# The last output product in two column halves, and which queues carry the last stores

## The chip, the cores and the metric

The kernel runs on one core of a Trainium2 chip. The metric is the time of one execution on the device in microseconds (us); the time before is the median of three runs. The profile belongs to one further execution, and its span, counted from the first instruction to the last, is a few microseconds shorter than the time.

## The reference

What is computed is a linear attention with a cosine weighting, followed by a feed-forward layer with a swish gate:

```python
q_p, k_p = phi(q, cos_w, sin_w), phi(k, cos_w, sin_w)      # relu(x)*cos, relu(x)*sin, side by side
kv  = np.einsum('bhsf,bhsd->bhfd', k_p, v)
num = np.einsum('bhsf,bhfd->bhsd', q_p, kv)
den = np.einsum('bhsf,bhf->bhs', q_p, k_p.sum(axis=2))[..., None] + 1e-06
x   = (num / den).transpose(0, 2, 1, 3).reshape(4608, 512)
h   = x @ w_in                                              # 4608 x 2048
out = (h * (1.0 / (1.0 + np.exp(-beta * h)))) @ w_out       # 4608 x 512, float32
```

There are 8 batches, 8 heads, 576 positions and 64 dimensions per head. Only the last product, `g @ w_out`, matters for the change.

## The kernel before

The 4608 rows of `x` are done in nine chunks of 512 rows (`c` from 0 to 8). For each chunk the first product and the gate give tiles `g_t` in bf16, and the second product multiplies them with `wout`. From chunk 2 on the second product is done by a fast 2 x 2 block scheme with seven block products instead of eight (`o_fast`). It works on a pair of row tiles of 128 rows, `pr` and `pr + 2`, and on two column halves of `HM` = 256 columns. The seven products are called 1 to 7; each is eight matmuls of 128 rows by 256 columns (line 552). They add up in three PSUM banks, `b_ps`, `e_ps` and `a_ps`. In between, ScalarE copies partial sums out (c1, c5, cu), and VectorE adds them to other banks (a2, a3, a7).

- `o1`, the upper row tile, is complete after a2 (left half, line 602) and a3 (right half, line 603).
- `o2`, the lower row tile, is complete after a7 (right half, line 604) and c4 (left half, line 571 to 576). Product 4 is the last one, and adds to `b_ps`, which c4 then copies.

Nothing reorders the work: the order in which the program issues it is written out by hand, in the strings `ORDER` and `ORDER_END`, which the function `chunk` walks through. `ORDER_END` is used for chunk 8. There `x` and `y` are the two calls of `o_fast`, and `oy3`, `o3y`, `oy4`, `c4y` at its end stand for product 3, a3, product 4 and c4 of the second pair. Each engine takes its instructions in that order, and waits on semaphores for data of the others. Two engines' accesses to the same PSUM bank are ordered one after the other by such waits too, even where they touch different columns.

A finished row tile is written to the output by `store` (line 512), in two transfers of 64 rows each, since each 64 rows belong to another place of the output. Chunks 0 to 6 use GpSimd's queue, the others SyncE's. In chunk 8 the odd row tiles, which are `o1` and `o2` of the second pair, use SyncE's queue for one transfer and ScalarE's for the other. The queue of an engine is in order too: ScalarE can't start a copy before it has issued the transfers that stand ahead of it.

For the last pair, c4 is cut in two: ScalarE copies columns 0 to 127 and VectorE columns 128 to 255 of the same bank, and then both transfers of the left half are issued. After the last store every engine goes through the closing instructions of the program, which the profile shows under line 1058: a drain, and a barrier in which SyncE waits for the transfers to land, and GpSimd gathers all engines.

Of the kernel before, what the change touches and what calls it, by code (L numbers as in the profile page):

```python
# [22 lines left out]
def kernel(  # L23
# [14 lines left out]
    nc = tc.nc  # L38

    B, H, S, D = q.shape  # L40
    DM = H * D
    DF = moe_w_in.shape[1]
    JT = DF // P
    MI = DM // P
    TCH = 512
    NTC = B * S // TCH
# [38 lines left out]
    HM = DM // 2  # L85
    w_e, w_o = wout[:, 0:JT:2], wout[:, 1:JT:2]
    B11, B12, B21, B22 = w_e[:, :, 0:HM], w_e[:, :, HM:DM], w_o[:, :, 0:HM], w_o[:, :, HM:DM]
    T1, T2, T4 = (const.tile([P, JT // 2, HM], BF16, name=f"T{i}") for i in (1, 2, 4))
# [420 lines left out]

    out_v = out.rearrange("(b p n) m -> b n p m", b=B, n=NQ)  # L510

    def store(c, tt, o_sb, m0=0, m1=DM):
        for hf in range(2):
            bb, n = divmod((c * TCH + tt * P) // HP + hf, NQ)
            eng = nc.gpsimd if c < 7 else (nc.sync, nc.scalar)[hf] if c == NTC - 1 and tt % 2 else nc.sync
            eng.dma_start(out=out_v[bb, n][:, m0:m1], in_=o_sb[hf * HP : (hf + 1) * HP, m0:m1])  # L516

    def o_mm(c, tt, jts, cols=1):
        o_ps = ps[:, (2, 3, 0, 1)[tt] if c == 0 else 2 + tt % 2]
        for jt in jts:  # L520
            w = DM // cols if jt > 0 else DM
            for m0 in range(0, DM, w):
                nc.tensor.matmul(o_ps[:, m0 : m0 + w], lhsT=gs[c, jt // 4][:, jt % 4, tt * P : (tt + 1) * P],  # L523
                                 rhs=wout[:, jt, m0 : m0 + w],
                                 start=(jt == 0), stop=(jt == JT - 1 and m0 == DM - w))
        if jts[-1] < JT - 1:
            return
        o_sb = osb_pool.tile([P, DM], FP32, name="o_sb", tag="o_sb")
        nc.scalar.copy(o_sb, o_ps)
        store(c, tt, o_sb)  # L530
# [6 lines left out]
    def late(c):  # L537
        made[c] = made.get(c, 0) + 1
        return made[c] > 14 - SPLITS.get(c, (0, 0))[1]

    def o_fast(c, pr, banks):

        b_ps, e_ps, a_ps = (ps[:, k_, 0:HM] for k_ in banks)
        tok = slice(pr * P, (pr + 1) * P)
        last = c == NTC - 1 and pr == 1

        def prod(dst, left, right, start, stop, pieces=False):
            order = (0, 1, 2, 3, 4, 5, 7, 6) if c + 1 >= B else range(JT // 2)
            for i in order:
                w = HM // 2 if i and pieces else HM  # L550
                for m in range(0, HM, w):
                    nc.tensor.matmul(dst[:, m : m + w], lhsT=left(i), rhs=right[:, i, m : m + w],  # L552
                                     start=start and i == 0,
                                     stop=stop and i == order[-1], skip_group_check=True)

        def g_part(r, hf):
            def at(i):
                jt = 2 * i + r
                return gs[c, jt // 4][:, jt % 4, hf * (TCH // 2) + pr * P : hf * (TCH // 2) + (pr + 1) * P]
            return at  # L560

        def s_part(t):
            return lambda i: t[:, i, tok]

        o1 = osb_pool.tile([P, DM], FP32, name="o_sb", tag="o_sb")
        o2 = osb_pool.tile([P, DM], FP32, name="o_sb", tag="o_sb")
        p1 = part.tile([P, HM], FP32, name="p1", tag="p1")
        p5 = part.tile([P, HM], FP32, name="p5", tag="p5")
        u = part.tile([P, HM], FP32, name="u", tag="u")

        def c4():
            h = HM // 2 if last else HM
            nc.scalar.copy(o2[:, 0:h], b_ps[:, 0:h])
            if last:
                nc.vector.tensor_copy(o2[:, h:HM], b_ps[:, h:HM])
                store(c, pr + 2, o2, 0, HM)

        def stored(key, op):
            def do():
                op()  # L580
                waits[key[0]].discard(key[1:])
                if not waits[key[0]] and not (last and key[0] == "2"):
                    store(c, pr + (2 if key[0] == "2" else 0), o2 if key[0] == "2" else o1)
                if last and key == "2a7":
                    store(c, pr + 2, o2, HM, DM)
            return do

        waits = {"1": {"a2", "a3"}, "2": {"a7", "c4"}}
        add = dict(op=ALU.add)
        return {  # L590
            "1": lambda: prod(b_ps, g_part(0, 0), B11, True, False, late(c)),
            "5": lambda: prod(e_ps, s_part(S1), T1, True, False, late(c)),
            "6": lambda: prod(b_ps, s_part(S2), T2, False, False, late(c)),
            "2": lambda: prod(a_ps, g_part(1, 0), B21, True, True, late(c)),
            "7": lambda: prod(b_ps, s_part(S3), T3, False, False, late(c)),
            "3": lambda: prod(e_ps, s_part(S4), B22, False, True, late(c)),
            "4": lambda: prod(b_ps, g_part(1, 1), T4, False, True, late(c)),
            "c1": lambda: nc.scalar.copy(p1, b_ps),
            "c5": lambda: nc.scalar.copy(p5, e_ps),
            "cu": lambda: nc.scalar.copy(u, b_ps),  # L600
            "c4": stored("2c4", c4),
            "a2": stored("1a2", lambda: nc.vector.tensor_tensor(o1[:, 0:HM], a_ps, p1, **add)),
            "a3": stored("1a3", lambda: nc.vector.tensor_tensor(o1[:, HM:DM], e_ps, u, **add)),  # L603
            "a7": stored("2a7", lambda: nc.vector.tensor_tensor(o2[:, HM:DM], b_ps, p5, **add)),
        }
# [16 lines left out]
    for bank, n0, n1 in ((6, 0, 5), (7, 5, NQ)):  # L622
        for n in range(n0, n1):
            nc.tensor.matmul(ps[:, bank, (n - n0) * HP : (n - n0 + 1) * HP],
                             lhsT=tan9[0:HP, n : n + 1].to_broadcast([HP, P]), rhs=identf,
# [357 lines left out]
    for c in range(2, NTC):  # L983
        b = c + 1
        parts = (6, 0, 4) if c < FAST else (0, 6, 4)
        xb, yb = ((2, 3, 6), (1 if c == FAST - 1 else 7, 3, 6)) if c < FAST else ((3, 2, 0), (1, 2, 0)) if b < B else ((0, 3, 6), (1, 3, 6))
        x, y = o_fast(c, 0, xb), o_fast(c, 1, yb)
        if c >= FAST:
            chunk(c, b, x, y, parts)
# [73 lines left out]
```

## Time and profile before

| | before |
|---|---|
| time, median of three (lowest, highest) | 280.73 us (279.52, 281.05) |
| span of the profiled execution | 278.1 us |
| granted TensorE clock | 0.999 |
| PE busy | 269.0 us, 97% |
| DVE busy | 209.6 us, 75% |
| ACT busy | 178.0 us, 64% |
| GpSimd busy | 71.1 us, 26% |
| stores of `o_sb` on GpSimd, SyncE, ScalarE | 56, 15, 3 |
| GpSimd's last store starts at | 226.4 us |

The busy time is the sum of an engine's instructions; issuing a transfer counts as busy on no engine but GpSimd. In the lines of the profile PE is the matmul, PEld its weight load, DVE is VectorE, ACT is ScalarE, POOL is GpSimd and SP is SyncE. A q behind an engine's name (SPq, ACTq) stands for its sequencer, which waits and issues transfers while the engine itself is idle. `L516` is line 516 of the kernel, where all output stores are issued, `out<-in` names what is written and read, and x4 counts instructions. Landing is the time at which the last byte of a transfer is known to have arrived.

### The profile page before, as it was taken

How to read it: one execution, taken by the hardware profiler on the slowest of the kernel's cores; microseconds unless marked ns; L12 is line 12 of the kernel's file. 1: busy time of each engine (PE TensorE's matmuls, PEld its weight loads, DVE VectorE, ACT ScalarE, POOL GpSimd, SP SyncE). 2: the span in 40 equal slices, each digit the busy share in tenths (PEclk: the TensorE clock that was granted, in tenths of full speed). 3: DMA queues.
4: the chain of work that ended last, by engine and by line, in shares of the span. 5: the costliest groups of instructions: out<-in, count | busy, mean ns of one | idle time of the engine just before them, and what ended most of it. 6: DMA issues, size and time to landing. Idle time of an engine off the chain costs nothing.

```text
span 278.1 us, 8732 instructions
## 1 busy us (share of the span) xinstructions
PE 269.0 (97%) x3613; PEld 191.8 (69%) x3619; DVE 209.6 (75%) x539; ACT 178.0 (64%) x348; POOL 71.1 (26%) x89
## 2 busy tenths in 40 slices
PE   7799999999999999999999999999999999999993
PEld 6354455445874588549854898788767886888783
DVE  5989968668999596358749995799679779659832
ACT  5778757773137657675767586896685279429911
POOL 1444000616192074106320542007400140000000
PEclk9999999999999999999999999999999999999999
DMA  6999999999989968992899189705400640033006
GB/s 242 377 394 382 392 391 305 367 204 396 213 261 295 266 193 219 384 177 42 184 373 241 35 211 277 147 21 106 116 2 12 116 113 4 0 76 78 0 4 150
DMA packets 50583, 53.98 MB, mean 194 GB/s; under 512 B 31200, under 2 KB 31472, under 8 KB 50544
## 3 DMA queue, kind: packets, MB, share of 16 engines
q1 hardware_dynamic: 47584, 45.82, 57.4%
q0 software_dynamic: 2688, 7.34, 9.0%
q8 instruction: 28, 0.46, 0.7%
q10 hardware_dynamic: 272, 0.27, 0.4%
q14 instruction: 11, 0.09, 0.2%
HBM read 36.71 MB, written 9.44 MB: 166 GB/s over the span
## 4 chain that ended last, share of the span: by engine, by line
PE 91%; DMA 3%; DVE 2%; SPq 1%; issue 1%; ACTq 0%; ACT 0%
PE ps L552 31%; PE ps L380 25%; PE ps L474 11%; PE ps L523 10%; PE ps L428 7%; PE ps L293 4%; DMA raw_v<-in_v_dram 3%; PE ps L272 3%; SPq L79 1%; DVE xs L315 1%; PE ps L234 0%; PE ps L352 0%; DVE win L115 0%; DVE rden L308 0%; DVE vb L209 0%
## 5 line engine op out<-in xcount | busy, mean ns | idle before, releaser
L380 PE MATMUL ps<-xt,win 128*128 128x512 bf16 (+1 forms) x327 | 71.1, 375 | 0.1
L388 ACT ACTIVATE g_t<-ps,beta 128x512 bf16<-128x512 f32 x80 | 54.6, 688 | 19.1 <-PE ps L380 17.9
L380 PEld LDWEIGHTS <-win 128*128 128x128 bf16 x327 | 31.4, 98 | 35.2 <-issue 0.4
L516 POOL DMA_DIRECT2D out_dram<-o_sb x56 | 31.7, 571 | 65.5 <-DVE o_sb L603 33.0
L552 PEld LDWEIGHTS <-S 128*128 128x128 bf16 x476 | 44.3, 98 | 4.7
L419 ACT ACTIVATE g_t<-ps,beta 128x512 bf16<-128x512 f32 x64 | 41.2, 697 | 3.4 <-PE ps L428 2.2
L552 PEld LDWEIGHTS <-g_t 128*128 128x128 bf16 x364 | 33.0, 98 | 3.6
L222 POOL TENSOR_TENSOR qs<-qt,tanr 128x1152 bf16<-128x1152 bf16 x8 | 19.4, 2447 | 46.9 <-DVE S L399 17.2
L399 DVE TENSOR_TENSOR S<-g_t 128x512 bf16<-128x512 bf16 (+1 forms) x62 | 22.3, 393 | 11.5 <-ACT g_t L388 9.1
L523 PE MATMUL ps<-wout,g_t 128*128 128x256 bf16 (+1 forms) x171 | 28.6, 318 | 0.4 <-issue 0.2
L552 PE MATMUL ps<-wout,g_t 128*128 128x256 bf16 (+1 forms) x238 | 28.1, 266 | 0.0
L552 PE MATMUL ps<-wout,S 128*128 128x256 bf16 (+1 forms) x238 | 27.4, 266 | 0.0
L552 PE MATMUL ps<-T,S 128*128 128x256 bf16 (+1 forms) x238 | 27.1, 266 | 0.0
L428 PE MATMUL ps<-xt,win 128*128 128x512 bf16 (+1 forms) x111 | 24.0, 350 | 0.0
L315 DVE TENSOR_TENSOR xs<-ps,rden 128x768 bf16<-128x768 f32 (+4 forms) x26 | 22.8, 884 | 0.8
L523 PEld LDWEIGHTS <-g_t 128*128 128x128 bf16 x177 | 16.9, 98 | 9.2
L219 DVE TENSOR_SCALAR vb<-raw_v,cos 128x256 bf16<-128x256 f32 x63 | 22.6, 417 | 0.0
L217 ACT ACTIVATE vb<-raw_v,sin 128x256 bf16<-128x256 f32 (+1 forms) x50 | 21.8, 498 | 0.8 <-DMA raw_v<-in_v_dram 0.8
L474 PE MATMUL ps<-w_stage 128*128 128x256 bf16 x120 | 20.3, 273 | 0.0
L474 PEld LDWEIGHTS <-w_stage 128*128 128x128 bf16 x160 | 15.5, 98 | 3.9
L222 POOL TENSOR_TENSOR w_stage<-qt,tanr 128x1152 bf16<-128x1152 bf16 x4 | 9.4, 2380 | 27.9 <-DVE den L304 27.9
L428 PEld LDWEIGHTS <-win 128*128 128x128 bf16 x111 | 10.9, 98 | 6.7
(104 smaller groups left out, 380.3 us busy)
## 6 DMA issues: line engine op xcount, KB each, us to landing
raw_v<-in_v_dram SPq DMA_DIRECT2D x7, 1152.0 KB, 10.6
raw_k<-in_k_dram SPq DMA_DIRECT2D x7, 1152.0 KB, 8.3
raw_q<-in_q_dram SPq DMA_DIRECT2D x7, 1152.0 KB, 8.0
out_dram<-o_sb POOLq DMA_DIRECT2D x56, 128.0 KB, 4.6
w_stage<-in_moe_w_in_dram SPq DMA_DIRECT2D x3, 1024.0 KB, 13.4
w_stage<-in_moe_w_out_dram SPq DMA_DIRECT2D x2, 1024.0 KB, 7.9
w_stage<-in_moe_w_out_dram SPq DMA_DIRECT2D x4, 512.0 KB, 12.0
out_dram<-o_sb SPq DMA_DIRECT2D x13, 128.0 KB, 2.4
```

What stands on the lines that cost most here:

```text
L219: nc.vector.tensor_scalar(o, a, scalar1=t[:, n : n + 1], scalar2=None, op0=ALU.mult)
L222: return eng.tensor_tensor(dst.rearrange("q n (g p) -> q n g p", g=2), src.rearrange("q n (g p) -> q n g p", g=2), tanr[:, n0:n1].unsqueez ...
L315: nc.vector.tensor_tensor(o.rearrange("q j n s d -> q j (n s) d"), nv[:, :, a:z, :, 0:D].rearrange("q j n s d -> q j (n s) d"), rden[:, :, ...
L380: nc.tensor.matmul(ps[:, h_bank(c, jt), i * 64 : (i + w) * 64], lhsT=win[jt // 4][:, mi, (jt % 4) * P : (jt % 4 + 1) * P], rhs=xt[:, i : i ...
L388: nc.scalar.activation(gs[c, jt // 4][:, jt % 4], ps[:, h_bank(c, jt)], AF.Silu, scale=beta[:, jt : jt + 1])
L399: return nc.vector.tensor_tensor(o, l, r, op=op)
L419: nc.scalar.activation(gs[c, jt // 4][:, jt % 4], ps[:, bank], AF.Silu, scale=beta[:, jt : jt + 1])
L428: nc.tensor.matmul(ps[:, bank, o * 64 : z * 64], lhsT=win[jt // 4][:, mi, (jt % 4) * P : (jt % 4 + 1) * P], rhs=xt[:, o:z, jp, g * HP : (g ...
L474: nc.tensor.matmul(dst, lhsT=left[:, g], rhs=right[:, :, g * HP : (g + 1) * HP], start=start and g == 0, stop=stop and g == 1, skip_group_ ...
L516: eng.dma_start(out=out_v[bb, n][:, m0:m1], in_=o_sb[hf * HP : (hf + 1) * HP, m0:m1])
L523: nc.tensor.matmul(o_ps[:, m0 : m0 + w], lhsT=gs[c, jt // 4][:, jt % 4, tt * P : (tt + 1) * P], rhs=wout[:, jt, m0 : m0 + w], start=(jt == ...
L552: nc.tensor.matmul(dst[:, m : m + w], lhsT=left(i), rhs=right[:, i, m : m + w], start=start and i == 0, stop=stop and i == order[-1], skip ...
```

## The change

The last product (product 4 of the second pair in chunk 8) is computed in two column halves of 128 columns: eight matmuls for columns 0 to 127, then VectorE copies these and they are stored, on SyncE's and GpSimd's queues; then eight matmuls for columns 128 to 255, which ScalarE copies, with stores on ScalarE's and SyncE's queues. It is for letting the copy and the store of the first half run while the second is still to be computed. The two stores of `o1` of that pair move to GpSimd's queue, so that SyncE's and ScalarE's queues are free for the last ones. The right half of `o2` keeps SyncE and ScalarE.

```diff
-    def store(c, tt, o_sb, m0=0, m1=DM):
+    def store(c, tt, o_sb, m0=0, m1=DM, engs=None):
         for hf in range(2):
             bb, n = divmod((c * TCH + tt * P) // HP + hf, NQ)
-            eng = nc.gpsimd if c < 7 else (nc.sync, nc.scalar)[hf] if c == NTC - 1 and tt % 2 else nc.sync
+            eng = nc.gpsimd if c < 7 else nc.sync
+            if engs:
+                eng = engs[hf]
...
-        def c4():
-            h = HM // 2 if last else HM
-            nc.scalar.copy(o2[:, 0:h], b_ps[:, 0:h])
-            if last:
-                nc.vector.tensor_copy(o2[:, h:HM], b_ps[:, h:HM])
-                store(c, pr + 2, o2, 0, HM)
-
         def stored(key, op):
             def do():
                 op()
                 waits[key[0]].discard(key[1:])
+                if last and key == "2a7":
+                    store(c, pr + 2, o2, HM, DM, (nc.sync, nc.scalar))
                 if not waits[key[0]] and not (last and key[0] == "2"):
-                    store(c, pr + (2 if key[0] == "2" else 0), o2 if key[0] == "2" else o1)
-                if last and key == "2a7":
-                    store(c, pr + 2, o2, HM, DM)
+                    store(c, pr + (2 if key[0] == "2" else 0), o2 if key[0] == "2" else o1,
+                          engs=(nc.gpsimd, nc.gpsimd) if last else None)
             return do
+
+        def prod_last():
+            left, right, h = g_part(1, 1), T4, HM // 2
+            for m in (0, h):
+                for i in range(JT // 2):
+                    nc.tensor.matmul(b_ps[:, m : m + h], lhsT=left(i), rhs=right[:, i, m : m + h], start=False,
+                                     stop=m > 0 and i == JT // 2 - 1, skip_group_check=True)
+                if m == 0:
+                    nc.vector.tensor_copy(o2[:, 0:h], b_ps[:, 0:h])
+                    store(c, pr + 2, o2, 0, h, (nc.sync, nc.gpsimd))
+
+        def copy_last():
+            h = HM // 2
+            nc.scalar.copy(o2[:, h:HM], b_ps[:, h:HM])
+            store(c, pr + 2, o2, h, HM, (nc.scalar, nc.sync))
...
-            "4": lambda: prod(b_ps, g_part(1, 1), T4, False, True, late(c)),
+            "4": prod_last if last else lambda: prod(b_ps, g_part(1, 1), T4, False, True, late(c)),
...
-            "c4": stored("2c4", c4),
+            "c4": copy_last if last else stored("2c4", lambda: nc.scalar.copy(o2[:, 0:HM], b_ps)),
```

## What I expected before the run

> **What bounds the kernel now.** I read the page first: PE is busy for 97% of the span at full granted clock, and the chain that ended last is 91% PE. So the body is TensorE's, and the change leaves it alone: every instruction before the last product is the same on every engine. All that can move is the stretch from the last product to the end of the span. I therefore read the chain of waits in order of time from 270 us on (start, length, what):
>
> ```profile
> 269.95 2.96 PE ps L552 x27
> 272.92 0.02 issue
> 272.94 0.44 DVE o_sb L603
> 273.38 0.02 issue
> 273.40 0.47 ACTq L516
> ...
> 274.04 0.28 ACT o_sb L573
> 274.32 0.02 issue
> 274.34 0.29 DVE o_sb L575
> ```
>
> The reader is to see that the last copies do not wait for PE. The last eight matmuls end at 273.78 (start 272.74 and 1.04 long in the timeline), yet ACT's copy starts at 274.04: ACT's own queue was issuing half of the o1 store (0.47 us), which in turn had waited for the DVE sum L603. Then DVE's copy waits for ACT's. Next, the stores of the end, from the timeline and from the answer for line 516 on SyncE's queue from 273.6 on:
>
> ```profile
> 272.98 2.57 SPq L516 DMA_DIRECT2D out_dram<-o_sb  x4
> ...
> 274.66 0.47 ACTq L516 DMA_DIRECT2D out_dram<-o_sb  x1
> ```
>
> ```profile
> L516 SPq DMA_DIRECT2D out_dram<-o_sb x3: 547/549/605, 273.7 to 275.0; - x3
> ...
> DMA to landing us min/median/max: 2.1/2.5/2.6
> ```
>
> SyncE issues back to back, some 0.65 us apart, so that its last store goes out at 275.0 though its data was ready at 274.63: about 0.35 us of backlog. It lands 2.1 us later, at 277.14; the span ends at 278.06, some 0.9 us after that, in the closing drains and semaphores of line 1058.
>
> Last, line 1058 on GpSimd, between 220 and 235 us, and GpSimd's timeline:
>
> ```profile
> L1058 POOLq DRAIN  x1: 5496/5496/5496, 226.2 to 226.2; - x1
> ```
>
> ```profile
> 223.84 3.08 POOL L516 DMA_DIRECT2D out_dram<-o_sb  x6 [4.24 <-DVE o_sb L603]
> ```
>
> This is the line that decides my forecast. GpSimd's last store starts at 226.40 and its record ends at 226.92. The closing drain behind it runs until 226.16 + 5.50 = 231.66: 4.73 us past the end of that record, and 2.3 us past the landing of the last store (226.4 + 2.9 = 229.3). Now it lies under 46 us of other engines' work and costs nothing. The two other drains of GpSimd, at the very end with no store before them, take 0.10 and 0.04 us.
>
> **What the Trainium skill says.** "DMA: Bandwidth & Descriptors", section "Issuing engines are not separate DMA queues": stores from several engines share the same DMA engines, and spreading them saves only the sequencer's issue time. The trace agrees: an issue takes 0.47 to 0.61 us on SyncE and ScalarE, and that is the backlog above. The same page, "Anatomy of one DMA — SWDGE (gpsimd) path", puts about 2.0 us of fixed cost on a GpSimd transfer, mostly the receipt of the write; the six stores from 223.8 on land after 2.2 to 2.9 us, SyncE's at the end after 2.1 to 2.6. "PSUM — Partial Sum Buffer", section "PSUM bank collisions raise a hardware error", wants accesses of two engines to one bank kept apart even at different columns; the trace shows it kept, DVE's copy of columns 128 to 256 waits for ACT's of 0 to 128. I found no page that prices GpSimd's drain behind stores.
>
> **The change part by part.**
>
> 1. *Product in halves.* 8 matmuls of 256 columns become 16 of 128. The trace has the small form: 28 of L552 on `g_t` take 1.9 us, starts 0.056 us apart, 0.219 us long each. The first half starts at 272.74 as before, and its end is 272.74 + 7 × 0.056 + 0.22 = 273.35. The DVE copy (0.291 us, the row L575 now) must wait for DVE's L603, which ends at 273.37, so it runs 273.39 to 273.68. Both halves lie in one bank, so the second half waits for that copy: PE idles for about 0.37 us. A matmul waiting for DVE started 0.02 to 0.05 us after DVE's end elsewhere in the trace, so the second half runs 273.73 to 274.34, and ACT's copy (0.266 us) from 274.38 to 274.65. Behind the waiting matmul PE has only these eight, and for them waits only ACT's copy. The last copy of before ended at 274.63: **plus 0.02 us**, nothing.
>
> 2. *o1's two stores leave SyncE and ScalarE.* ScalarE's copy no longer sits behind its own issue (that is in step 1), and SyncE loses one of its four closing issues. SyncE now has: right part until 274.17, left quarter (ready at 273.68) 274.22 to 274.77, last quarter from 274.82. Before it was 275.0: **minus 0.18 us**. ScalarE's last quarter goes at 274.69. With 2.1 to 2.5 us to land, SyncE's side ends at 276.9 to 277.3 against 277.14: the span would move by −0.2 to +0.2 us.
>
> 3. *Three stores on GpSimd.* o1's two wait for L603 at 273.37 and go at 273.40 and 273.97; the lower half of the left quarter has its data at 273.68, but queued behind them it goes at about 274.49, record over at 275.0 (0.52 to 0.58 us each, the trace's rows). Landing at +2.2 to +3.4 (the least and the most of its last eight stores): 276.7 to 277.9, 277.1 with the median of 2.6. On its own that is −0.2 to +0.7 us on the span.
>
> 4. *GpSimd's closing drain moves.* It cannot end before the engine is done with its last store, and the closing barrier needs it. The trace shows one such drain only, so I bound it. Low end: it costs as much as the drains without stores, 0.1 us, and step 3's landing sets the end. High end: the 4.73 us past the last record repeat, 275.0 + 4.73 = 279.73. Between: 2.3 us past the landing, 277.1 + 2.3 = 279.4. I take the middle of the last two, 279.57, because nothing else in GpSimd's stream lies between that store and the drain's end, and because the drains without stores are short. From GpSimd's arrival to the end of the span the trace shows 277.33 to 278.06, 0.73 us: 280.30. Sum: 280.30 − 278.06 = **plus 2.24 us**, and steps 1 and 2 lie beneath it. On 280.73 us that is 282.97, 0.8% more.
>
> No cost: the DVE copy for ACT's, and four quarter stores for two half ones, same bytes, with the DMA engines empty after 277 us in either case.
>
> **The rivals.**
>
> *The drain bounds the end* (my forecast): for it, the 5.50 us row; against it, it is one sample, behind six stores close together, and here there are three. 282.6 (2.3 us past an early landing) to 283.3.
>
> *The drain is short or overlaps the landing.* For it: ACT's own closing drain ends 0.48 us after its store's issue and does not wait for the landing. Then the later of SyncE's and GpSimd's landings sets the end: −0.1 to +0.7 us, likeliest no difference, 280.8. Within 0.5%.
>
> *The end gets faster.* If the second half did not wait for the copy, PE would be done by 273.8, ACT's copy at 274.1, all stores out by 274.4 but for SyncE's queue; with the barrier that saves 0.4 to 0.6 us, 280.2, and that is still inside 0.5%. Past 0.5%, 279.3, I see only the scatter of the runs (279.52 to 281.05 before). The wait of the second half on DVE speaks against it.
>
> *GpSimd is slower to start after 47 idle us*: some stores landed 5 to 7.7 us after issue in the crowded middle of the kernel. Here the DMA engines are nearly free, so little chance; then the end is at 274.5 + 6 + 2.3 + 0.7 = 283.5 on the span, 286 in time.
>
> **How the numbers follow.** The drain 0.73, the drain short 0.18, the faster end 0.06, the slow start 0.03. The time is the drain's: 283.0. The drain's own bounds are 282.6 to 283.3, with 0.3% of scatter 282.2 to 283.8; without the second case more than 2 in 10 would be left out, so the range goes down to 280.5 and ends at 283.8. Slower 0.75 (drain, slow start), same 0.19, faster 0.06.
>
> **What would show it.** Step 1: a gap of 0.3 to 0.4 us on PE before the last eight matmuls, and ACT's last copy ending near 274.65. Step 2: SyncE's last store issued near 274.8, landing near 277.1. Step 3: three GpSimd stores from 273.4 on, the last landing near 277. Step 4: a GpSimd drain of 4 us or more at the end, ending near 279.5, with all landings done two microseconds earlier. The forecast is wrong if that drain ends before 277.5, and if the span then ends within 1 us of the last landing.

## The result, and the profile after

The changed kernel takes 283.52 us (median of six runs, 282.52 to 283.61) against 280.63 us before (six runs, 279.52 to 281.05). The ratio is 1.0102, with a 95% interval of 1.0079 to 1.0124: it is slower, by 2.9 us.

The span of the profiled execution is 281.7 us, 3.6 longer than before. Of these, 0.8 us were there ahead of the last product (the DVE sum that completes `o1` starts at 273.75 instead of 272.94), where both kernels have the same instructions; the profiled run of before, 279.85 us, was 0.8 below its own median too. So I compare what follows that sum: from its start to the end of the span it is 5.12 us before and 7.93 us after, 2.81 us more. That is nearly the whole of the 2.9 us.

The chain of waits of the kernel after, from 273 us on (start, length, what). Lines of before move by eleven in that part of the code: 603 is now 614, 1058 is 1069, and stores are on line 518:

```profile
273.75 0.43 DVE o_sb L614
274.18 0.28 issue
274.46 0.45 POOL out_dram L518
274.91 0.07 issue
274.98 0.52 POOL out_dram L518
275.50 0.51 POOLq L1069
```

ScalarE's queue and the two copies are gone from it. In their place stand GpSimd's stores, and then line 1069 on GpSimd, its closing drain. This view stops at 276.01, where GpSimd's last store ends, and doesn't follow the drain to its end. The view of the closing line does. Each row gives the count, then least, median and greatest length in ns, then first and last start. First the kernel before, where the line is 1058:

```profile
L1058 POOLq EVENT_SEMAPHORE  x4: 17/17/17, 277.3 to 278.0; - x4
L1058 POOLq DRAIN  x3: 40/102/5496, 226.2 to 277.8; - x3
L1058 SPq DRAIN  x3: 7/7/13, 277.2 to 277.5; - x3
```

Then the kernel after:

```profile
L1069 POOLq EVENT_SEMAPHORE  x4: 17/17/17, 280.9 to 281.6; - x4
L1069 POOLq DRAIN  x3: 40/102/5509, 275.4 to 281.4; - x3
L1069 SPq DRAIN  x3: 7/7/13, 278.8 to 281.2; - x3
```

The first start in GpSimd's semaphore row is where it gathers the engines. Before, that was 277.3, right after SyncE had seen all its landings (277.2). After, SyncE is as far at 278.8, but GpSimd gathers only at 280.9, right behind its own drain: the long one of the three, which starts at 275.4 and ends at 280.90. The drain's record begins even before the last store's does, so its length is no measure of the wait; I count from the end of the last store's record. The timeline of the same stretch shows how the two halves went (the brackets give idle time and what ended it):

```profile
273.55 0.61 PE L588 MATMUL ps<-T,g_t 128*128 128x128 bf16 x8
...
274.19 0.29 DVE L591 COPY o_sb<-ps 128x128 f32<-128x128 f32 x1
274.46 1.54 POOL L518 DMA_DIRECT2D out_dram<-o_sb  x3 [46.74 <-DVE o_sb L614]
274.54 0.61 PE L588 MATMUL ps<-T,g_t 128*128 128x128 bf16 x8 [0.38 <-DVE o_sb L591]
...
275.18 0.27 ACT L596 COPY o_sb<-ps 128x128 f32<-128x128 f32 x1 [1.94 <-PE ps L588]
```

PE idles 0.38 us between the halves, waiting for the copy. GpSimd starts its first store 0.29 us after the DVE sum ends and its last record ends at 276.01. The drain ends 4.89 us later, and the span 0.78 us after that. The last transfer of all lands at 278.70, 2.2 us ahead of the drain's end.

The last two stores on SyncE, from 275.05 us on, show a thing that I had not expected:

```profile
L518 SPq DMA_DIRECT2D out_dram<-o_sb x2: 546/550/553, 275.1 to 275.8; - x2
...
DMA to landing us min/median/max: 2.9/3.1/3.3
```

They are issued nearly as early as I had hoped, but take 2.9 and 3.3 us to land, where the last three of before took 2.1 to 2.6.

### The profile page after: what moved, and what is told of

It is laid out like the page before. It is cut to its first block, busy times and chain, and to the rows that moved or that the text cites. A ratio compares the mean times of both kernels' runs of the same rounds, so it can differ in the third digit from the quotient of the medians.

```text
span 281.7 us, 8752 instructions
## 1 busy us (share of the span) xinstructions
PE 271.1 (96%) x3621; PEld 193.5 (69%) x3627; DVE 209.4 (74%) x539; ACT 177.7 (63%) x348; POOL 72.2 (26%) x92
## 4 chain that ended last, share of the span: by engine, by line
PE 85%; DMA 9%; DVE 2%; SPq 1%; issue 1%; POOL 0%; POOLq 0%
PE ps L554 30%; PE ps L380 22%; PE ps L474 11%; PE ps L525 7%; PE ps L428 7%; DMA raw_q<-in_q_dram 6%; PE ps L293 4%; DMA raw_v<-in_v_dram 3%; PE ps L272 2%; SPq L79 1%; DVE xs L315 1%; PE ps L234 0%; PE ps L352 0%; DVE win L115 0%; DVE vb L209 0%
## 5 line engine op out<-in xcount | busy, mean ns | idle before, releaser
L518 POOL DMA_DIRECT2D out_dram<-o_sb x59 | 33.2, 569 | 113.4 <-DVE o_sb L614 79.6
L554 PEld LDWEIGHTS <-g_t 128*128 128x128 bf16 x356 | 32.2, 98 | 3.5
L525 PEld LDWEIGHTS <-g_t 128*128 128x128 bf16 x177 | 16.9, 98 | 9.2
```

## The experiments

All start either from the kernel before or from the one after. For each I give the time against the kernel before on the same chip, and the tail: from the start of the DVE sum that completes the last `o1` to the end of the span, 5.12 us before and 7.93 after. Beside the first four experiments the kernel before took 280.12 us (median of 17 runs), beside the later ones with a ratio 280.51 us (median of 43). A tail, and every time inside it, is read from one profiled execution.

### The column halves without GpSimd

```diff
-                          engs=(nc.gpsimd, nc.gpsimd) if last else None)
+                          engs=(nc.sync, nc.scalar) if last else None)
...
-                    store(c, pr + 2, o2, 0, h, (nc.sync, nc.gpsimd))
+                    store(c, pr + 2, o2, 0, h, (nc.sync, nc.scalar))
```

> The change without GpSimd: the last product in two column halves, each copied and stored by itself, but o1's stores on SyncE and ScalarE as before, and the left quarter on SyncE and ScalarE. Theory (GpSimd's closing drain carries the whole loss): the time is that of before within 0.3 to 0.5 us, 280.6 to 281.2, a few tenths over it because SyncE now issues five closing stores. No GpSimd drain above 0.2 us after 270 us. Rival (the wait of the second half on the copy, or four small stores in place of two, carries a good part of it): 281.8 or more.

It took 281.07 us, ratio 1.0035 (1.0014 to 1.0055), so about 1 us more than before. The tail is 6.06 us, 0.93 more. So without GpSimd two thirds of the loss are gone, but the halves cost more than the 0.3 to 0.5 us that I had expected. Two things are seen in the trace. SyncE has five stores to issue, and the last goes out 2.72 us after the start of the DVE sum, where it was 2.07 before. The last landing comes 0.57 us later for it. And the time from the last landing to the end of the span is 1.29 us instead of 0.92. SyncE's closing waits are as many as before, nine, but they stand in a fixed order. Before, the last transfer to land was the one waited for last; here it is waited for third, and six more waits follow, one after the other. The last ends 0.41 us past the landing instead of 0.05. The view of them from the last landing on, before and here:

```profile
L1058 SPq EVENT_SEMAPHORE  x1: 28/28/28, 277.2 to 277.2; - x1
```

```profile
L1069 SPq EVENT_SEMAPHORE  x7: 28/28/28, 278.0 to 278.4; - x7
```

Besides, ScalarE's copy ends at 275.27, 2.03 us after the start of that sum, against 1.69 for the last copy of before, again because ScalarE's queue issues stores ahead of it. The last three quarter stores land quickly here, 1.9 to 2.1 us after their issue (the first took 2.5 us); the view of SyncE's stores from 275.2 on:

```profile
L518 SPq DMA_DIRECT2D out_dram<-o_sb x3: 552/616/743, 274.6 to 276.0; - x3
...
DMA to landing us min/median/max: 2.0/2.1/2.4
```

### The stores on GpSimd without the column halves

```diff
+            if c == NTC - 1 and tt == 1:
+                eng = nc.gpsimd
```

> The kernel before with only o1's two closing stores on GpSimd; the last product whole. Theory: GpSimd's second store is over about 1.3 us after the DVE sum of line 603 ends, its drain ends 4.8 us later, the barrier takes 0.75: plus 2.2 to 2.4 us on the kernel before, 282.8 to 283.1. Rival (GpSimd's stores only land late): the end follows the landing, plus 0 to 0.7 us.

282.86 us, ratio 1.0109 (1.0093 to 1.0125); the tail is 7.55 us, 2.43 more than before (2.7 by the two medians). This part of the change does most of the damage by itself. The view of the closing line on GpSimd, 1060 in this kernel:

```profile
L1060 POOLq DRAIN  x3: 40/93/5639, 274.7 to 280.8; - x3
```

Its drain ends 5.03 us past the end of the last store's record (275.28 to 280.31), and 2.4 us past that store's landing.

### One store on GpSimd

```diff
+            if c == NTC - 1 and tt == 1 and hf == 1:
+                eng = nc.gpsimd
```

> The kernel before with one of o1's two closing stores on GpSimd. Theory (the drain lasts a fixed 4.7 to 4.9 us past the end of the last store's record, however many stores): the record is over 0.5 us earlier than with two, so plus 1.7 to 1.9 us on the kernel before, and a drain of about 5.4 us. Rival (the drain pays per store that is outstanding, some 1.6 us each with three): the drain ends before the last landing of SyncE's stores and the time is that of before, or less by 0.2 us since SyncE has one store less to issue.

281.61 us, ratio 1.0068 (1.0051 to 1.0085): 1.4 to 2.4 us more by that interval, 1.5 by the two medians; the tail is 1.62 us longer. I had expected 1.7 to 1.9.

```profile
L1060 POOLq DRAIN  x3: 40/93/5274, 274.3 to 280.1; - x3
```

One store has nearly the same drain as two or three: it ends 4.73 us past the end of the store's record, against 5.03 and 4.89. It only starts one record earlier. So the drain does not pay by the store.

### Two stores on GpSimd, 3.4 us earlier

```diff
+            if c == NTC - 1 and tt == 0:
+                eng = nc.gpsimd
```

> The kernel before with the two stores of the row tile before (o1 of the first pair of chunk 8, ready 3.4 us before the last pair's o1) on GpSimd. Theory: the drain is as long, 5.4 us, but ends some 1 to 2 us ahead of the last landing of SyncE's stores, so the time is that of before within 0.3 us. Rival (any store of GpSimd after the 46 idle us costs 2 us, by waking it or by its own barrier work): plus 1.5 us or more.

280.06 us, ratio 1.0001 (0.9988 to 1.0014): nothing.

```profile
L1060 POOLq DRAIN  x3: 40/93/5427, 270.5 to 277.8; - x3
```

The long drain is there, 4.81 us past the last record's end, but it ends at 275.92, and SyncE's waits for the landings run until 277.2 anyway. So it is the drain's place in time that costs, and not GpSimd's being woken after long idling.

### A late landing behind the stores

```diff
             store(c, pr + 2, o2, h, HM, (nc.scalar, nc.sync))
+            nc.gpsimd.dma_start(out=raws["q", B - 1][:, 0:4].rearrange("q j n d -> q j (n d)"),
+                                in_=q[B - 1].rearrange("(j g) (p n) d -> (g p) j (n d)", g=2, n=NQ))
```

> The changed kernel with one more transfer behind its last store on GpSimd's queue: 1152 KB of q loaded again into a tile that nothing reads any more (the output is the reference's). It lands 4 to 7 us after its issue, where the stores landed after 2.3 to 3.0. Theory A (the drain counts from the engine's last issue): it ends 4.7 to 5.1 us past the end of the load's record, whatever the landing, possibly before the landing plus 1 us. Theory B (the drain counts from the last landing): it ends 2.3 to 2.7 us after the landing of the load, so 6.5 us or more past the end of its record, and the span grows by 3 us or more.

```profile
L1071 POOLq DRAIN  x3: 40/102/9444, 275.1 to 285.1; - x3
```

The load's record ends at 275.92 and it lands at 282.05; the drain ends at 284.55. That is 8.64 us past the record and 2.50 past the landing, as theory B has it. With stores, the last of which landed 2.4 to 3.1 us after its issue, both rules give nearly the same end, which is why the earlier runs could not tell them apart. The load is also nine times as large as a store, and that its size and not its landing made the drain longer was not tested. (One run, 287.11 us.)

### An operation behind the last store

```diff
             store(c, pr + 2, o2, h, HM, (nc.scalar, nc.sync))
+            nc.gpsimd.memset(warm, 0.0)
```

> The changed kernel with a memset of one column on GpSimd behind its last store, which waits for nothing. If only the drain waits for what the stores left behind, the memset starts within 0.2 us of the end of the last store's record, and drain and span are those of the changed kernel within 0.3 us. If the engine itself is taken for 4.8 us after a store, the memset starts 4 us or more after it, and the drain ends right behind it.

283.62 us in one run. GpSimd's timeline:

```profile
274.50 1.55 POOL L518 DMA_DIRECT2D out_dram<-o_sb  x3 [46.72 <-DVE o_sb L615]
276.04 0.12 POOL L598 MEMSET warm<- 128x1 f32 x1
```

The memset follows at once, and the drain still ends 5.02 us past the store's record. The engine is free for work after a store; only the drain waits.

### Late work on GpSimd without a store

```diff
+        def a3():
+            nc.vector.tensor_tensor(o1[:, HM:DM], e_ps, u, op=ALU.add)
+            if last:
+                for i in range(3):
+                    nc.gpsimd.tensor_copy(eps9[:, i : i + 1], o1[:, DM - 1 - i : DM - i])
...
-            "a3": stored("1a3", lambda: nc.vector.tensor_tensor(o1[:, HM:DM], e_ps, u, **add)),
+            "a3": stored("1a3", a3),
```

> The kernel before with three copies of one column on GpSimd that read o1 after the DVE sum of line 603, and no store there: late work on GpSimd without a transfer. Theory (the drain's length comes from the stores): the drain ends within 0.2 us of the last copy, and the time is that of before within 0.3 us. Rival (any late work of GpSimd, after 46 idle us, makes the closing drain 5 us long): plus 1.5 us or more.

This went against my theory: 281.43 us, ratio 1.0034 (1.0019 to 1.0049), 0.9 us more, and a tail 1.24 us longer. GpSimd's timeline, and its closing line:

```profile
275.17 0.42 POOL L592 COPY eps<-o_sb 128x1 f32<-128x1 f32 x3 [46.50 <-DVE o_sb L589]
```

```profile
L1064 POOLq DRAIN  x3: 40/102/5104, 275.2 to 280.8; - x3
```

The drain ends 4.66 us past the last of three tiny copies, although GpSimd's last store was issued more than 46 us earlier. It does not need a recent store to be long.

### The same with no transfer of GpSimd in the whole kernel

```diff
-            eng = nc.gpsimd if c < 7 else (nc.sync, nc.scalar)[hf] if c == NTC - 1 and tt % 2 else nc.sync
+            eng = nc.sync if c < 7 else (nc.sync, nc.scalar)[hf] if c == NTC - 1 and tt % 2 else nc.sync
```

> Late copies of one column on GpSimd as in the run before, but now with all of GpSimd's 56 stores on SyncE's queue, so that GpSimd issues no transfer in the whole kernel. (SyncE's queue is in order, so the body may be slower; only the closing drain is read.) Late work without a store there still had a drain of 4.66 us past the last copy, against my expectation of 0.2. Theory A (the first drain after any use of GpSimd's transfers costs 4.7 us, even 46 us later): the drain now ends within 0.2 us of the last copy. Theory B (GpSimd's closing drain always takes about 4.7 us past its last instruction, transfers or not): it still ends 4.5 to 5 us after the last copy.

```profile
275.28 0.42 POOL L592 COPY eps<-o_sb 128x1 f32<-128x1 f32 x3 [81.77 <-DVE o_sb L589]
```

```profile
L1064 POOLq DRAIN  x3: 40/78/508, 275.3 to 279.6; - x3
```

Same copies, same wait, and the drain is 0.51 us long, over 0.07 us after the last copy. So in these two runs the 4.7 us belong to a GpSimd that has issued transfers in the kernel, and are paid at its first drain after them, here with the last one issued 47 us before. (One run, 282.07 us, with the last sum starting at 274.8: the time is not compared, since SyncE carries 56 more stores there.)

### A version meant to beat both

```diff
-            eng = nc.gpsimd if c < 7 else (nc.sync, nc.scalar)[hf] if c == NTC - 1 and tt % 2 else nc.sync
+            eng = nc.gpsimd if c < 7 else (nc.sync, nc.scalar)[hf] if c == NTC - 1 and tt % 2 else nc.sync
+            if c == NTC - 1 and tt == 3 and m0 > 0:
+                eng = nc.scalar
...
-            h = HM // 2 if last else HM
-            nc.scalar.copy(o2[:, 0:h], b_ps[:, 0:h])
             if last:
-                nc.vector.tensor_copy(o2[:, h:HM], b_ps[:, h:HM])
+                nc.vector.tensor_copy(o2[:, 0:HM], b_ps)
                 store(c, pr + 2, o2, 0, HM)
+            else:
+                nc.scalar.copy(o2[:, 0:HM], b_ps)
```

> A version that may beat both: the kernel before, with the last product whole, its left half copied by VectorE alone (0.41 us for 256 columns) so that ScalarE's issue of o1's store no longer stands ahead of the last copy, and both stores of the right half on ScalarE's queue, so that SyncE has two closing issues less ahead of the last one. No store on GpSimd. Theory (the end of before is the issue backlog plus the serial copies): the last copy ends 0.4 us earlier, at 274.25 on the span of before, the last store goes out at 274.3 instead of 275.0, and the time falls by 0.4 to 0.7 us, 0.15 to 0.25%. Rival (landing sets the end whatever the issue): no change.

280.46 us, ratio 0.9997 (0.9981 to 1.0012): no difference that can be measured. My theory failed, and the rival came out. The profile shows where the gain went. The last copy ends 1.30 us after the start of the DVE sum instead of 1.69, and the last store is issued after 1.37 us instead of 2.07. But it lands 3.99 us after that start instead of 4.20: the closing stores are now issued close together, and the last two take 2.5 and 2.6 us to land instead of 2.3 and 2.1. Of 0.7 us gained at the issue, 0.2 are left in the tail (4.89 us). The two stores of `o1` ahead of them took 2.8 and 2.9 us. The views of SyncE's store of `o1` and of its last store:

```profile
DMA to landing us min/median/max: 2.9/2.9/2.9
```

```profile
DMA to landing us min/median/max: 2.6/2.6/2.6
```

## Why the prediction was right

It named the one thing that decided, from one line of the trace: GpSimd's closing drain, hidden before, ends the kernel after. Each part of the change alone shows it: with GpSimd's stores alone the tail grows by 2.43 us, with the column halves alone by 0.93, and both together make it 2.81.

- **Step 1, the halves.** Right. PE idled 0.38 us (0.37 forecast), and the last copy ended 1.70 us after the start of the DVE sum, against 1.69 before: plus 0.01, forecast plus 0.02.
- **Step 2, SyncE's side.** The issue was nearly right: SyncE's last store went out 2.01 us after that start, 0.06 earlier than before (0.18 forecast). But SyncE does not lose one of its four closing issues, as I wrote: it gives up a half of `o1`, but its part of the left half becomes two quarters, so it issues four before and after. The landing was wrong. I had 2.1 to 2.5 us and no change of the span; it was 2.9 to 3.3, and the last landing came 0.75 us later than before. In the trace these stores land one after the other behind GpSimd's second store, which took 3.0 us: at 278.00, 278.19, 278.36, 278.53 and 278.70. With only `o1` on GpSimd the last ones took 3.0 and 3.2 us, with one store on GpSimd 2.1 to 2.5. But GpSimd isn't needed for it: in the version meant to beat both, with no store on GpSimd at the end, the two stores of `o1` took 2.8 and 2.9 us. That the stores stand closer together in these runs is a rival that no run separates. The drain covers this, so it cost nothing here.
- **Step 3, GpSimd's stores.** Three, as forecast, but the first starts 0.29 us after the DVE sum and not 0.03. The trace of before had this number: GpSimd's store at 223.84 starts 0.29 us after the DVE sum that it waits for. The end of the last record came 2.26 us after the sum's start and not 2.06. That is 0.20 us of the difference.
- **Step 4, the drain.** Right in kind and short in size: I took 4.57 us past the record, the mean of two readings of one sample; it was 4.89. That is 0.32 us, and the closing barrier another 0.05. Together with step 3: 0.57 us, which is 2.81 less the 2.24 of the forecast. The two bounds given for the drain, 282.6 and 283.3, don't follow from the sums shown: 2.3 us past the earliest landing of step 3 gives 282.4, and 4.73 us past the record gives 283.1. The measured 283.52 lies above either pair, and inside the range by the scatter that was added.
- **The reason given for step 4** was only partly right. I took the drain to be long because of the stores just ahead of it. The runs show two conditions, each of them on one trace. A GpSimd that has issued transfers earlier drains 4.7 us past its last instruction, even when its stores had landed 44 us before; and where a large load lands late, the drain ends 2.5 us past that landing. For stores that land after 2.4 to 3.1 us the two readings give nearly the same end, so that I could take their mean without knowing which holds: to that extent the number is luck. What the engine does in these 4.7 us was not seen in any trace.
- **The rivals.** The short drain is ruled out by every run with GpSimd's stores at the end, the slow start by the stores that landed in 2.2 to 2.5 us after 43 idle us. The faster end, as the rival has it, did not come: the second half did wait for the copy. Another way to it, with the product whole, gained 0.2 us in one tail, which the times can't tell from zero.

There is a second cost that I had put at nothing: the column halves cost about 1 us when their stores stay on SyncE and ScalarE, by a longer queue and by the place of the last landing in the order of the closing waits. In the changed kernel such a cost lies beneath the drain: SyncE is done with its waits at 278.8, 2 us ahead of the drain's end.

## What to carry to other kernels

Look for the closing drain of each engine in the profile, not only for the landings: an engine's last work is over when its drain is, and for a GpSimd that has issued transfers that was 4.7 to 5.0 us after its last instruction here, and more behind a load that landed late. Let GpSimd finish early, or give the last stores to the other queues: with two stores that were ready 3.4 us earlier, GpSimd's last record ended 5.9 us ahead of the last landing, and the cost was gone. At the very end of a kernel, each further small store also costs an issue of about 0.6 us on its queue, so cutting the last piece in halves can pay only where that issue is not the limit; no run here shows it paying.

## What the hardware showed that I had not expected

- The drain of GpSimd after three copies of one column: it ended 4.66 us past the last copy when GpSimd had issued 56 stores earlier, 0.07 us past it when GpSimd had issued none.
- With a load that landed after 6.9 us, the drain ended 2.50 us past the landing; with stores it ended 2.3 to 2.8 us past theirs.
- The last stores land one after another, 0.17 to 0.19 us apart, behind a larger store that was issued before them, in the kernel before (276.81, 276.98, 277.14) as in the one after. SyncE's and ScalarE's stores issued behind the second one of GpSimd took 2.9 to 3.4 us to land, without GpSimd at the end 1.9 to 2.9. Why the larger store ahead took 2.5 us before (SyncE's) and 3.0 after (GpSimd's) was not settled.
